# Single PSUM banks in place of pairs for the Fourier products, a third bank for the W_in product, and later uses of what went through DRAM

## The chip, the cores and the metric

One core of a Trainium2 chip runs the kernel as one program. The metric is the device time of one execution in microseconds (us); the kernel before takes 2753.14 us in the median of three runs. TensorE is the matmul engine, VectorE (DVE), ScalarE (ACT) and GpSimd (POOL) work on tiles, and SyncE (SP) issues most of the DMAs. PSUM is the accumulator memory: eight banks of 512 fp32 columns on 128 partitions.

## What is computed

A Fourier layer feeds a mixture-like MLP. With x of 8 batches, 3008 positions and 256 channels, and F = 2048:

```python
X = np.fft.rfft(x, axis=1)
Yr = Xr @ w_r - Xi @ w_i + b_r
Yi = Xr @ w_i + Xi @ w_r + b_i
Yr = np.sign(Yr) * np.maximum(np.abs(Yr) - lam, 0.0)
Yi = np.sign(Yi) * np.maximum(np.abs(Yi) - lam, 0.0)
y = np.fft.irfft(Y, n=x.shape[1], axis=1)
h = y @ w_in
g = h * np.cos(h)
out = g @ w_out
```

## The kernel before, in words

3008 is 64 x 47, so the real transform is done as two small ones (64 and 47 points, the latter padded to 48). For one batch the Fourier layer has three stages. stage_a (L354) makes the 64-point transform, tile pa, and sends it to DRAM (scr1). stage_b (L383) reads it back (tile at) in four quarters q: f2t1 (L410) makes the 47-point transform pb and splits it into a high and a low part Xh, Xl; wmix (L472) makes the three products pw with the Fourier weights, adds, clips, and at its end calls fold (L540) for both halves e, which combines rows on GpSimd, transposes on VectorE and sends the result through DRAM (scrT) into y; inverse, that is spread (L574), makes the 47-point inverse pi and stores it to DRAM (scr2). stage_c (L661) reads 1/6 of that back (tile bt), makes the 64-point inverse pc and evicts it as xTh and xTl, the input of the MLP.

The MLP (moe_step, L707) goes over 6 tiles t of 512 positions (the last 448) and 16 blocks f of 128 of the 2048 features. Each step has six matmuls into ph (h), ScalarE and VectorE make u = h cos h, gh and gl are its high and low part, and three steps later `second` (L689) adds six matmuls into two banks o0 and o1. It is 12 matmuls a step, 96 steps a batch.

The Fourier work of batch b + 1 and b + 2 is mixed into the MLP of batch b. The generators yield a cost; pull() (L817) runs after each half step and takes as much of the generator `ahead` (L779) as a fixed rate allows. The rate of tile t is (C_COST + share)/15/2 per pull, with C_COST = 5.22 and share = (A_COST + B_COST)/4.8 = 62.36/4.8. The yields inside stage_b stand for time that a DRAM round trip takes: 3.5 at its start, 2.0 ahead of wmix(0) (L649), 2.0 ahead of inverse(3) (L655); GAP = 5 units stand ahead of stage_c(b + 1, 0) (L799), and 3.5 between the load and the products of stage_c (L671). From this program the framework makes a fixed order for each engine: it takes instructions by the program's order, but puts a later one first where an earlier one is not expected to be ready; a buffer or bank is handed out when its first user is placed. `high_priority` moves an instruction to the front, `issue_after` keeps instructions behind a given one.

PSUM: tag f has two tiles of two banks each (`pair`, L284), for pa, pb, pw, pi and pc; tag h has two single banks for ph; o0 and o1 one each. The prologue's single tiles go round over six places, f, h, o0, f, h, o1 (fps, L276). pa and pi come in quartets: four small fp32 products, of two halves h of the input rows and two halves v of the output rows, that fill a pair and run side by side on the array (burst, L287); h says which bank.

Of the kernel before, what the change touches and what calls it, by code (L numbers as in the profile page):

```python
# [12 lines left out]
F32 = mybir.dt.float32  # L13
# [5 lines left out]
ALU = mybir.AluOpType  # L19
# [18 lines left out]
F2_COST = 0.43  # L38
GAP = 5
A_EVERY, A_FIRST = 3, 13  # L40
A_PAIR = 1.15
# [99 lines left out]
def tile_body(ctx: ExitStack, tc, x, w_r, w_i, b_r, b_i, w_in, w_out,  # L141
              c_f2, c_sig, c_f3, c_ff, c_if, c_iw, c_sgn, out):
    nc = tc.nc
# [210 lines left out]
    def stage_a(b):  # L354
        scr1[b] = dr.tile([32, 2, 2, 24, 256], F32, tag="scr1", name=f"scr1_{b}")
        ld = {}

        def load(c):
            if c < 12:
                ld[c] = stage_in("xt")  # L360
                with tc.issue_after(mark["f0", 2].ins) if b == 1 else ExitStack():
                    nc.sync.dma_start(ld[c], x[b, :, 512 * c:512 * (c + 1)])

        for c in range(2):
            load(c)
        yield 0.0
        yield 1.0
        for cc in range(6):
            p = pair("pa")
            xs = [ld.pop(2 * cc + v) for v in range(2)]  # L370
            burst([((p[64 * v:64 * v + 64, h], ff[64 * h:64 * h + 64, 256:], xs[v][64 * h:64 * h + 64]),
                    dict(start=True, stop=True, skip_group_check=True)) for v in (1, 0) for h in range(2)])
            ao = stage_out("ao")
            nc.scalar.copy(ao, p.rearrange("p h x -> p (h x)"))
            for v in range(2):
                i = 4 * cc + 2 * v
                nc.sync.dma_start(scr1[b][:, :, :, i:i + 2].rearrange("s r g i d -> (s r) g (i d)"),
                                  ao[64 * v:64 * v + 64].rearrange("p (g x) -> p g x", g=2))
                load(2 * cc + 2 + v)
            yield A_PAIR  # L380


    def stage_b(b):  # L383
# [26 lines left out]
        def f2t1(q):  # L410
# [10 lines left out]
            for hf in range(4):  # L421
# [11 lines left out]
                if b:  # L433
                    at = ld.pop(u)
                    if hf % 2 == 0:
                        p = pair("pb")
                    pv = p[:, hf % 2, :384].rearrange("p (s r c k) -> p s r c k", s=2, r=2, c=2)
                    for j in range(2):
                        for c in range(2):
                            mm(pv[:, j, :, c], at[:, j, 128 * c:128 * c + 128], f2[:, 2 * (hf % 2) + j],  # L440
                               start=j == 0 and c == 0, stop=j == 1 and c == 1, skip_group_check=True)
                    if hf % 2 == 0:
                        continue
                    pv = p[:, :, :384]
                    xhv, xlv = (a[:, 2 * hf - 2:2 * hf + 2].rearrange("p (u s) g k -> p u (s g k)", u=2) for a in (xh, xl))
# [26 lines left out]
        def wmix(q):  # L472
# [3 lines left out]
            if b:  # L476
                k1 = wk.tile([128, 2, 8, 48], F32, tag="k1", name="k1", bufs=1)
                for wj, comp in ((0, 2), (1, 0), (2, 1)):
                    p = pair("pw")
                    for e in range(2):  # L480
                        es = slice(128 * e, 128 * e + 128)
                        for c in range(2):
                            xhv, xlv = (x[comp][c] for x in xs)
                            mm(p[:, e, :384], wf[:, wj, 0, c, es], xhv, start=c == 0, stop=False)  # L484
                            mm(p[:, e, :384], wf[:, wj, 1, c, es], xhv, start=False, stop=False)  # L485
                            mm(p[:, e, :384], wf[:, wj, 0, c, es], xlv, start=False, stop=c == 1)  # L486
                    p4 = p[:, :, :384].rearrange("p e (s k) -> p e s k", k=48)
                    if wj == 0:
                        nc.scalar.copy(k1, p4)
                        yield 2.0  # L490
                        continue
                    r = 2 - wj
                    sv = st[:, :, :, r, :]
                    if r:
                        nc.vector.tensor_tensor(out=sv, in0=p4, in1=k1, op=ALU.add)
                    else:
                        nc.vector.tensor_tensor(out=sv, in0=k1, in1=p4, op=ALU.subtract)
                    cl = wk.tile([128, 2, 8, 48], F32, tag="cl", name="cl", bufs=1)
                    for e in range(2):
                        nc.vector.tensor_scalar(out=cl[:, e], in0=sv[:, e], scalar1=blo[:, r, e:e + 1],  # L500
                                                scalar2=bhi[:, r, e:e + 1], op0=ALU.max, op1=ALU.min)
                    nc.vector.tensor_tensor(out=sv, in0=sv, in1=cl, op=ALU.subtract)
                    yield 2.0
                for e in range(2):
                    fold(q, e)
                return
            for e in range(2):
                es = slice(128 * e, 128 * e + 128)
                k1 = wk.tile([128, 8, 48], F32, tag="k1", name="k1", bufs=1)
                for wj, comp in ((0, 2), (1, 0), (2, 1)):  # L510
                    p = fps("pw")
                    pv = p[:, :384]
                    for c in range(2):
                        mm(pv, ws[wj][:, 256 * c + 128 * e:256 * c + 128 * e + 128],
                           xs[:, comp, c].rearrange("p s k -> p (s k)"), start=c == 0, stop=c == 1)
                    p3 = pv.rearrange("p (s k) -> p s k", k=48)
                    if wj == 0:
                        nc.scalar.copy(k1, p3)
                        yield 1.0
                        continue  # L520
                    r = 2 - wj
                    sv = st[:, e, :, r, :]
                    if r:
                        nc.vector.tensor_tensor(out=sv, in0=p3, in1=k1, op=ALU.add)
                    else:
                        nc.vector.tensor_tensor(out=sv, in0=k1, in1=p3, op=ALU.subtract)
                    cl = wk.tile([128, 8, 48], F32, tag="cl", name="cl", bufs=1)
                    if q < 3 and r == 0:
# [7 lines left out]
                    (nc.gpsimd if q < 3 else nc.vector).tensor_tensor(out=sv, in0=sv, in1=cl, op=ALU.subtract)  # L536
                    yield 1.0
        Y = {}
# [35 lines left out]
        def spread(q):  # L574
            y = Y.pop(q).rearrange("p (a s e) -> p a s e", a=8, s=8)
            for u in range(2):
                p = pair("pi")
                burst([((p[64 * v:64 * v + 64, h], iw[64 * h:64 * h + 55],
                         y[64 * h:64 * h + 55, :, 4 * u + 2 * v:4 * u + 2 * v + 2]),
                        dict(start=True, stop=True, skip_group_check=True)) for v in range(2) for h in (1, 0)])  # L580
                bo = stage_out("bo")
                for h in range(2):
                    nc.scalar.copy(bo[:, 512 * h:512 * h + 512].rearrange("p (s a e) -> p s a e", s=2, a=8),
                                   p[:, h].rearrange("p (a s e) -> p s a e", s=2, a=8))
# [64 lines left out]
        yield 2.0  # L649
# [5 lines left out]
        yield 2.0  # L655
# [5 lines left out]
    def stage_c(b, t):  # L661
# [10 lines left out]
        p = pair("pc")  # L672
        for hf in range(2):
            for j in range(2):
                for c in range(2):
                    o = 256 * j + 128 * c
                    mm(p[:, hf, o:o + 128], bt[:, 2 * hf + j, 128 * c:128 * c + 128], ff[:, 128:256], start=o == 0, stop=o == 384,  # L677
                       skip_group_check=True)
# [97 lines left out]
    B_COST = 4 * (8 * F2_COST + 6 * 1.0 + 2 * A_PAIR) + 7.5  # L776
# [88 lines left out]
```

## Time and profile before

| what | value |
|---|---|
| runs | 2750.15, 2753.14, 2754.5 us |
| profiled execution | 2753.34 us, of it a span of 2751.6 us from the first to the last instruction |
| TensorE busy | 2673.5 us (97%), mean granted clock 0.991 |
| VectorE, ScalarE, GpSimd busy | 1763.5, 1670.5, 988.7 us |
| TensorE idle | 78.1 us, the span less the busy time |

TensorE's records overlap: a matmul of 512 columns is recorded with about 390 ns, but the next one starts 0.23 us after it, and that distance is what a matmul costs. An fp32 product (pa, pb, pi, pc) has two records, one for each of its passes. A wait is listed as the idle time of an engine just before an instruction, with what ended it.

### The profile page before, as it was taken

To read this page: it belongs to the slowest core of one execution; us is meant where nothing else is said; L and a number is where in the kernel's file an instruction comes from. 1 tells how busy PE (TensorE), PEld (TensorE's weight loads), DVE (VectorE), ACT (ScalarE), POOL (GpSimd) and SP (SyncE) were. 2 spreads that over 40 slices of the span, in tenths; PEclk is the share of its full clock that TensorE was granted. 3 is DMA by queue.
4 is the path that set the end of the run, shared out by engine and by line. 5 is a ranking of instruction groups with operands and counts; after the bars stand their busy time and mean duration, and the time that the engine had idled before them with its cause. 6 is when DMAs were issued, how large, how long until landed. Compare 5 with 4: busy or idle time off the path is not lost.

```text
span 2751.6 us, 36096 instructions
## 1 busy us (share of the span) xinstructions
PE 2673.5 (97%) x13161; PEld 2186.7 (79%) x13161; DVE 1763.5 (64%) x2640; ACT 1670.5 (61%) x2846; POOL 988.7 (36%) x907
## 2 busy tenths in 40 slices
PE   8789999999999999999999999999999999999999
PEld 6467778878788877977878787887878778788888
DVE  6586565666666666666656666566665666666665
ACT  5465556666566656666666666666665555666666
POOL 4354343443233432444324343243423434222222
PEclk9999999999999999999999999999999999999999
DMA  6523422343213432133322432223331222201000
GB/s 195 149 76 104 127 90 80 90 120 108 73 34 96 120 94 73 40 116 111 92 62 77 113 105 81 62 84 104 94 92 40 73 68 58 81 16 30 8 16 15
DMA packets 148051, 224.89 MB, mean 82 GB/s; under 512 B 13840, under 2 KB 91168, under 8 KB 147872
## 3 DMA queue, kind: packets, MB, share of 16 engines
q1 hardware_dynamic: 142592, 205.24, 25.9%
q0 software_dynamic: 5280, 17.33, 2.1%
q8 instruction: 104, 1.70, 0.3%
q14 instruction: 75, 0.61, 0.1%
HBM read 121.33 MB, written 101.19 MB: 81 GB/s over the span
## 4 chain that ended last, share of the span: by engine, by line
PE 81%; DMA 8%; DVE 6%; issue 2%; ACT 1%; POOL 1%; SPq 1%; ACTq 0%; DVEq 0%; POOLq 0%
PE po L696 11%; PE ph L714 11%; PE po L700 11%; PE ph L715 11%; PE ph L716 11%; PE po L697 11%; PE pc L677 3%; DMA scrT<-tr 3%; DMA y<-scrT 3%; PE pb L440 3%; PE pw L486 2%; PE pw L485 2%; PE pw L484 2%; PE pi L290 2%; PE pa L290 1%
## 5 line engine op out<-in xcount | busy, mean ns | idle before, releaser
L267 POOL TENSOR_TENSOR gl<-u,gh 128x512 fp32r<-128x512 f32 (+1 forms) x384 | 487.5, 1270 | 1379.4 <-ACT gh L726 1055.4
L722 DVE SCALAR_TENSOR_TENSOR u<-ph,u 128x512 f32<-128x512 f32 (+1 forms) x768 | 518.8, 676 | 500.8 <-ACT u L721 497.8
L721 ACT ACTIVATE u<-ph 128x512 int32<-128x512 f32 (+1 forms) x768 | 451.2, 588 | 461.7 <-PE ph L716 454.8
L725 DVE TENSOR_TENSOR u<-ph,u 128x512 f32<-128x512 f32 (+1 forms) x768 | 520.2, 677 | 262.4 <-ACT u L724 245.4
L724 ACT ACTIVATE u<-u 128x512 f32<-128x512 f32 (+1 forms) x768 | 479.9, 625 | 288.2 <-DVE u L722 285.2
L714 PE MATMUL ph<-xTh,win 128*128 128x512 f32 (+1 forms) x1536 | 608.5, 396 | 7.1 <-DVE u L725 5.7
L696 PE MATMUL po<-gh,wout 128*128 128x512 f32 (+1 forms) x1536 | 603.5, 393 | 0.1
L715 PE MATMUL ph<-xTl,win 128*128 128x512 f32 (+1 forms) x1536 | 595.6, 388 | 0.0
L716 PE MATMUL ph<-xTh,win 128*128 128x512 f32 (+1 forms) x1536 | 595.2, 388 | 0.0
L697 PE MATMUL po<-gh,wout 128*128 128x512 f32 (+1 forms) x1536 | 594.2, 387 | 0.0
L726 ACT CAST gh<-u 128x512 fp32r<-128x512 f32 (+1 forms) x768 | 467.9, 609 | 195.2 <-DVE u L725 190.2
L700 PE MATMUL po<-gl,wout 128*128 128x512 f32 (+1 forms) x1536 | 482.2, 392 | 4.4 <-DVE gl L270 4.2
L696 PEld LDWEIGHTS po<-gh,wout 128*128 128x128 f32 x1536 | 289.6, 189 | 90.0 <-ACT u L721 30.0
L714 PEld LDWEIGHTS ph<-xTh,win 128*128 128x128 f32 x1536 | 289.7, 189 | 80.4 <-DVE u L725 18.0
L270 DVE TENSOR_TENSOR gl<-u,gh 128x512 fp32r<-128x512 f32 (+1 forms) x384 | 310.1, 808 | 52.3 <-ACT gh L726 45.7
L700 PEld LDWEIGHTS po<-gl,wout 128*128 128x128 f32 x1536 | 281.2, 188 | 74.2 <-issue 8.9
L716 PEld LDWEIGHTS ph<-xTh,win 128*128 128x128 f32 x1536 | 289.5, 188 | 57.6 <-issue 0.8
L697 PEld LDWEIGHTS po<-gh,wout 128*128 128x128 f32 x1536 | 289.5, 188 | 51.4
L715 PEld LDWEIGHTS ph<-xTl,win 128*128 128x128 f32 x1536 | 290.0, 189 | 49.4 <-issue 0.8
L677 PEld LDWEIGHTS pc<-ff,bt 128*128 128x128 f32 x768 | 105.5, 200 | 36.2 <-issue 17.9
L677 PE MATMUL pc<-ff,bt 128*128 128x128 f32 x768 | 108.4, 285 | 25.4 <-DMA bt<-scr 25.4
L440 PEld LDWEIGHTS pb<-f,at 96*128 96x128 f32 x896 | 116.6, 191 | 8.4
(120 smaller groups left out, 2460.4 us busy)
## 6 DMA issues: line engine op xcount, KB each, us to landing
scrT<-tr SPq DMA_DIRECT2D x56, 512.0 KB, 2.9
y<-scrT SPq DMA_DIRECT2D x112, 256.0 KB, 5.1
scr<-bo SPq DMA_DIRECT2D x128, 192.0 KB, 2.9
bt<-scr SPq DMA_DIRECT2D x96, 256.0 KB, 3.8
xt<-in_dram SPq DMA_DIRECT2D x84, 256.0 KB, 3.9
scr<-ao SPq DMA_DIRECT2D x84, 256.0 KB, 3.5
at<-scr SPq DMA_DIRECT2D x112, 192.0 KB, 3.1
out_dram<-ob SPq DMA_DIRECT2D x80, 256.0 KB, 2.2
```

The source lines that it names most:

```text
L267: return nc.gpsimd.tensor_tensor(out=lo, in0=x, in1=hi.bitcast(F32), op=ALU.subtract)
L696: mm(po[e][:, :n], wo[0][:, 0, f, es], gh[:, :n], start=f == 0, stop=False)
L697: mm(po[e][:, :n], wo[0][:, 1, f, es], gh[:, :n], start=False, stop=False)
L700: mm(po[e][:, :n], wo[0][:, 0, f, es], gl[:, :n], start=False, stop=f == NFC - 1)
L714: mm(h, win[:, 0, c, fs], th[:, c, :n], start=c == 0, stop=False)
L715: mm(h, win[:, 0, c, fs], tl[:, c, :n], start=False, stop=False)
L716: mm(h, win[:, 1, c, fs], th[:, c, :n], start=False, stop=c == 1)
L721: nc.scalar.activation(k[:, :n], h, AF.Identity, bias=0.25, scale=1.0 / TWO_PI)
L722: nc.vector.scalar_tensor_tensor(out=u[:, :n], in0=h, scalar=1.0 / TWO_PI, in1=k[:, :n], op0=ALU.mult, op1=ALU.subtract)
L724: nc.scalar.activation(u[:, :n], u[:, :n], AF.Sin, bias=HALF_PI, scale=TWO_PI)
L725: nc.vector.tensor_tensor(out=u[:, :n], in0=h, in1=u[:, :n], op=ALU.mult)
L726: nc.scalar.copy(gh[:, :n], u[:, :n])
```

## The change

PSUM is dealt out anew: tag f gets three single banks and tag h three, o0 and o1 stay. Each of pa and pi is two single tiles, one for each h; pb and pc are one single tile for each hf, and pw one for each half e, each with its own evictions (two of 512 or 384 columns in place of one of 1024 or 768). In a quartet the order of the four products is by h first, then v; before it was by v first. The first matmul of a quartet is no longer at high priority, and outside the prologue it waits for the readers of the fourth-last f tile, which are noted by `drained`; the other three stay at high priority behind it. wmix of the later batches runs over e outermost, with fold(q, e) right after each e; k1 and cl have two buffers in place of one and half the size. The prologue's single tiles go round over eight places. The yields become 3.0 ahead of wmix(0), 5.0 ahead of inverse(3), GAP 7; B_COST grows by the same 4.0; A_EVERY is 5 in place of 3, as stage_b now yields more often.

```diff
-GAP = 5
-A_EVERY, A_FIRST = 3, 13
+GAP = 7
+A_EVERY, A_FIRST = 5, 13
...
     def fps(name):
-        if not banks:
-            banks.extend(("f", "h", "o0", "f", "h", "o1"))
-        tag = banks.pop(0)
-        if tag == "f":
-            return pair(name)[:, 0]
-        return ps.tile([128, 512], F32, tag=tag, name=name, bufs=1 if tag[0] == "o" else 2)
-
-    def pair(name):
-        return ps.tile([128, 2, 512], F32, tag="f", name=name, bufs=2)
+        if "pro" in pool:
+            if not banks:
+                banks.extend(("f", "h", "o0", "f", "h", "o1", "f", "h"))
+            tag = banks.pop(0)
+            return ps.tile([128, 512], F32, tag=tag, name=name, bufs=1 if tag[0] == "o" else 3)
+        p = ps.tile([128, 512], F32, tag="f", name=name, bufs=3)
+        ring.append((p, []))
+        return p
+
+    ring = []
+
+    def drained(p, ins):
+
+        for q, readers in ring[-6:]:
+            if q is p:
+                readers.append(ins.ins)
 
     def burst(calls):
 
-        with tc.high_priority():
-            ins = mm(*calls[0][0], **calls[0][1])
-            with tc.issue_after(ins.ins):
-                for a, k in calls[1:]:
-                    mm(*a, **k)
+        ins = mm(*calls[0][0], **calls[0][1])
+        if len(ring) > 3:
+            for r in ring[-4][1]:
+                tc.add_manual_dep(ins.ins, r.name, mybir.DependencyInfo(
+                    mybir.DependencyClass.Sync, mybir.DependencyReason.DATA), reason="bank")
+        with tc.high_priority(), tc.issue_after(ins.ins):
+            for a, k in calls[1:]:
+                mm(*a, **k)
...
-            p = pair("pa")
+            p = [fps("pa") for _ in range(2)]
...
-                    dict(start=True, stop=True, skip_group_check=True)) for v in (1, 0) for h in range(2)])
+                    dict(start=True, stop=True, skip_group_check=True)) for h in range(2) for v in (1, 0)])
             ao = stage_out("ao")
-            nc.scalar.copy(ao, p.rearrange("p h x -> p (h x)"))
+            for h in range(2):
+                drained(p[h], nc.scalar.copy(ao[:, 512 * h:512 * h + 512], p[h]))
...
-                    if hf % 2 == 0:
-                        p = pair("pb")
-                    pv = p[:, hf % 2, :384].rearrange("p (s r c k) -> p s r c k", s=2, r=2, c=2)
+                    p = fps("pb")
+                    pv = p[:, :384].rearrange("p (s r c k) -> p s r c k", s=2, r=2, c=2)
...
                     nc.scalar.copy(xhv, pv)
-                    nc.vector.tensor_tensor(out=xlv, in0=pv, in1=xhv.bitcast(F32), op=ALU.subtract)
-                    yield 4 * F2_COST
+                    drained(p, nc.vector.tensor_tensor(out=xlv, in0=pv, in1=xhv.bitcast(F32), op=ALU.subtract))
+                    if hf % 2:
+                        yield 4 * F2_COST
                     continue
...
-            if b:
-                k1 = wk.tile([128, 2, 8, 48], F32, tag="k1", name="k1", bufs=1)
-                for wj, comp in ((0, 2), (1, 0), (2, 1)):
-                    p = pair("pw")
...
-                for e in range(2):
-                    fold(q, e)
-                return
             for e in range(2):
                 es = slice(128 * e, 128 * e + 128)
-                k1 = wk.tile([128, 8, 48], F32, tag="k1", name="k1", bufs=1)
+                k1 = wk.tile([128, 8, 48], F32, tag="k1", name="k1", bufs=2)
...
+                        xhv, xlv = (x[comp][c] for x in xs)
+                        mm(pv, wf[:, wj, 0, c, es], xhv, start=c == 0, stop=False)
+                        mm(pv, wf[:, wj, 1, c, es], xhv, start=False, stop=False)
+                        mm(pv, wf[:, wj, 0, c, es], xlv, start=False, stop=c == 1)
...
                     yield 1.0
+                if b:
+                    fold(q, e)
...
-                p = pair("pi")
+                p = {h: fps("pi") for h in (1, 0)}
...
-                        dict(start=True, stop=True, skip_group_check=True)) for v in range(2) for h in (1, 0)])
+                        dict(start=True, stop=True, skip_group_check=True)) for h in (1, 0) for v in range(2)])
...
-        yield 2.0
+        yield 3.0
         yield from wmix(0)
...
-        yield 2.0
+        yield 5.0
         yield from inverse(3)
...
-        p = pair("pc")
         for hf in range(2):
+            p = fps("pc")
...
-        pv = p.rearrange("p f (j c n) -> p c (f j) n", j=2, c=2)
-        thv, tlv = (a.rearrange("p c (i n) -> p c i n", i=4) for a in (th, tl))
-        nc.scalar.copy(thv, pv)
-        nc.vector.tensor_tensor(out=tlv, in0=pv, in1=thv.bitcast(F32), op=ALU.subtract)
+            pv = p.rearrange("p (j c n) -> p c j n", j=2, c=2)
+            thv, tlv = (a[:, :, 256 * hf:256 * hf + 256].rearrange("p c (j n) -> p c j n", j=2) for a in (th, tl))
+            nc.scalar.copy(thv, pv)
+            drained(p, nc.vector.tensor_tensor(out=tlv, in0=pv, in1=thv.bitcast(F32), op=ALU.subtract))
...
-        ph = ps.tile([128, 512], F32, tag="h", name="ph", bufs=2)
+        ph = ps.tile([128, 512], F32, tag="h", name="ph", bufs=3)
...
-    B_COST = 4 * (8 * F2_COST + 6 * 1.0 + 2 * A_PAIR) + 7.5
+    B_COST = 4 * (8 * F2_COST + 6 * 1.0 + 2 * A_PAIR) + 11.5
```

## Rows read from the trace of the kernel before

**Rows 1.** The page: busy us, share of the span, instructions of each engine.
```profile
PE 2673.5 (97%) x13161; PEld 2186.7 (79%) x13161; DVE 1763.5 (64%) x2640; ACT 1670.5 (61%) x2846; POOL 988.7 (36%) x907
```

**Rows 2.** Stretches: busy us of each engine over one batch, granted clock, DMA.
```profile
core 0: us, PE busy (x) PEld busy (x) DVE busy (x) ACT busy (x) POOL busy (x), PEclk, DMA share, GB/s
...
780.00:1110.00 330.00, 326.73 (x1631) 267.58 (x1630) 213.41 (x318) 202.12 (x344) 122.67 (x112) 1.00 0.30 87
```

**Rows 3.** TensorE's waits, whole run: us in total, times, longest.
```profile
PE pc L677 <- DMA bt<-scr: 25.4, 8, 11.4
PE pi L290 <- DMA y<-scrT: 18.5, 12, 3.7
PE ph L714 <- DVE u L725: 5.7, 8, 1.6
PE po L700 <- DVE gl L270: 4.2, 4, 1.2
...
PE pi L619 <- ACT bo L622: 1.4, 1, 1.4
```

**Rows 4.** Stretches at half clock in the steady part: first, last, sum of six.
```profile
302.70:306.10 3.40, 3.40 (x11) 2.83 (x12) 0.28 (x1) 1.59 (x3) 3.05 (x2) 0.50 0.27 61
...
2381.40:2384.90 3.50, 3.50 (x16) 3.31 (x16) 0.62 (x1) 0.62 (x1) 1.27 (x1) 0.51 0.02 5
sum 23.90, PE 23.60 PEld 18.49 DVE 3.12 ACT 6.99 POOL 9.60; mean PE 3.93 PEld 3.08 DVE 0.52 ACT 1.16 POOL 1.60
```

**Rows 5.** Timelines of SP's queue and of PE around one bt wait.
```profile
1066.95 1.27 SPq L669 DMA_DIRECT2D bt<-scr  x2
...
1069.35 0.39 PE L716 MATMUL ph<-xTh,win 128*128 128x512 f32 x1
1071.93 1.80 PE L677 MATMUL pc<-ff,bt 128*128 128x128 f32 x14 [2.20 <-DMA bt<-scr]
```

**Rows 6.** Timelines of PE and ACT: a pc group, later work, its eviction.
```profile
1080.65 1.95 PE L677 MATMUL pc<-ff,bt 128*128 128x128 f32 x16
...
1111.79 1.92 PE L440 MATMUL pb<-f,at 96*128 96x96 f32 x16
...
1158.11 1.01 ACT L681 CAST xTh<-pc 128x1024 fp32r<-128x1024 f32 x1
```

**Rows 7.** Timelines of PE and its weight loads around one quartet.
```profile
1003.82 0.39 PE L715 MATMUL ph<-xTl,win 128*128 128x512 f32 x1
...
1004.04 0.39 PE L716 MATMUL ph<-xTh,win 128*128 128x512 f32 x1
...
1004.36 0.64 PE L290 MATMUL pi<-y,iw 55*64 55x512 f32 x1
1004.37 0.14 PEld L293 LDWEIGHTS pi<-y,iw 55*64 55x64 f32 x3
1004.37 0.65 PE L293 MATMUL pi<-y,iw 55*64 55x512 f32 x3
...
1004.84 0.59 PE L290 MATMUL pi<-y,iw 55*64 55x512 f32 x1
...
1005.38 0.50 PE L696 MATMUL po<-gh,wout 128*128 128x512 f32 x1
```

**Rows 8.** TensorE's y waits in 450 to 2103 us, then in 2103 to 2440 us.
```profile
PE pi L290 <- DMA y<-scrT: 4.1, 5, 1.1
...
PE pi L290 <- DMA y<-scrT: 9.4, 4, 3.7
```

**Rows 9.** Groups by shape of ACT and DVE: busy us, mean ns of one.
```profile
L583 ACT COPY bo<-pi 128x512 f32<-128x512 f32 x112 | 59.3, 583 | 13.5 <-PE pi L293 13.4
...
L374 ACT COPY ao<-pa 128x1024 f32<-128x1024 f32 x42 | 42.3, 1007 | 3.7 <-PE pa L293 3.6
...
L725 DVE TENSOR_TENSOR u<-ph,u 128x512 f32<-128x512 f32 x640 | 440.5, 688 | 218.7 <-ACT u L724 205.8
...
L682 DVE TENSOR_TENSOR xTl<-pc,xTh 128x1024 fp32r<-128x1024 f32 x48 | 58.8, 1224 | 13.8 <-ACT xTh L681 13.8
```

**Rows 10.** Groups by shape of PE: the first product of each quartet, two records each.
```profile
L290 PE MATMUL pi<-y,iw 55*64 55x512 f32 x112 | 60.4, 621 | 18.5 <-DMA y<-scrT 18.5
L290 PE MATMUL pa<-xt,ff 64*64 64x512 f32 x84 | 44.9, 614 | 1.1 <-DVE Xl L447 1.1
```

More of the change, by code (lines that the diff above doesn't have):

```diff
@@ L368, in stage_a @@
         for cc in range(6):
-            p = pair("pa")
+            p = [fps("pa") for _ in range(2)]
             xs = [ld.pop(2 * cc + v) for v in range(2)]
-            burst([((p[64 * v:64 * v + 64, h], ff[64 * h:64 * h + 64, 256:], xs[v][64 * h:64 * h + 64]),
-                    dict(start=True, stop=True, skip_group_check=True)) for v in (1, 0) for h in range(2)])
+            burst([((p[h][64 * v:64 * v + 64], ff[64 * h:64 * h + 64, 256:], xs[v][64 * h:64 * h + 64]),
+                    dict(start=True, stop=True, skip_group_check=True)) for h in range(2) for v in (1, 0)])
             ao = stage_out("ao")
-            nc.scalar.copy(ao, p.rearrange("p h x -> p (h x)"))
+            for h in range(2):
+                drained(p[h], nc.scalar.copy(ao[:, 512 * h:512 * h + 512], p[h]))
             for v in range(2):
@@ L441, in f2t1 @@
                                start=j == 0 and c == 0, stop=j == 1 and c == 1, skip_group_check=True)
[L442 to L445, printed above, removed]
+                    pv = p[:, :384]
+                    xhv, xlv = (a[:, 2 * hf:2 * hf + 2].rearrange("p s g k -> p (s g k)") for a in (xh, xl))
                     nc.scalar.copy(xhv, pv)
-                    nc.vector.tensor_tensor(out=xlv, in0=pv, in1=xhv.bitcast(F32), op=ALU.subtract)
-                    yield 4 * F2_COST
+                    drained(p, nc.vector.tensor_tensor(out=xlv, in0=pv, in1=xhv.bitcast(F32), op=ALU.subtract))
+                    if hf % 2:
+                        yield 4 * F2_COST
                     continue
@@ L475, in wmix @@
             ST[q] = st
-            if b:
-                k1 = wk.tile([128, 2, 8, 48], F32, tag="k1", name="k1", bufs=1)
-                for wj, comp in ((0, 2), (1, 0), (2, 1)):
-                    p = pair("pw")
-                    for e in range(2):
[L481 to L489, printed above, removed]
-                        yield 2.0
[L491 to L502, printed above, removed]
-                    yield 2.0
-                for e in range(2):
-                    fold(q, e)
-                return
             for e in range(2):
                 es = slice(128 * e, 128 * e + 128)
-                k1 = wk.tile([128, 8, 48], F32, tag="k1", name="k1", bufs=1)
+                k1 = wk.tile([128, 8, 48], F32, tag="k1", name="k1", bufs=2)
                 for wj, comp in ((0, 2), (1, 0), (2, 1)):
@@ L513, in wmix @@
                     for c in range(2):
-                        mm(pv, ws[wj][:, 256 * c + 128 * e:256 * c + 128 * e + 128],
-                           xs[:, comp, c].rearrange("p s k -> p (s k)"), start=c == 0, stop=c == 1)
+                        if b == 0:
+                            mm(pv, ws[wj][:, 256 * c + 128 * e:256 * c + 128 * e + 128],
+                               xs[:, comp, c].rearrange("p s k -> p (s k)"), start=c == 0, stop=c == 1)
+                            continue
+                        xhv, xlv = (x[comp][c] for x in xs)
+                        mm(pv, wf[:, wj, 0, c, es], xhv, start=c == 0, stop=False)
+                        mm(pv, wf[:, wj, 1, c, es], xhv, start=False, stop=False)
+                        mm(pv, wf[:, wj, 0, c, es], xlv, start=False, stop=c == 1)
                     p3 = pv.rearrange("p (s k) -> p s k", k=48)
                     if wj == 0:
-                        nc.scalar.copy(k1, p3)
+                        drained(p, nc.scalar.copy(k1, p3))
                         yield 1.0
@@ L523, in wmix @@
                     if r:
-                        nc.vector.tensor_tensor(out=sv, in0=p3, in1=k1, op=ALU.add)
+                        i = nc.vector.tensor_tensor(out=sv, in0=p3, in1=k1, op=ALU.add)
                     else:
-                        nc.vector.tensor_tensor(out=sv, in0=k1, in1=p3, op=ALU.subtract)
-                    cl = wk.tile([128, 8, 48], F32, tag="cl", name="cl", bufs=1)
-                    if q < 3 and r == 0:
+                        i = nc.vector.tensor_tensor(out=sv, in0=k1, in1=p3, op=ALU.subtract)
+                    drained(p, i)
+                    cl = wk.tile([128, 8, 48], F32, tag="cl", name="cl", bufs=2)
+                    if b == 0 and q < 3 and r == 0:
                         nc.scalar.activation(cl, sv, AF.Relu, bias=blo[:, r, e:e + 1], scale=-1.0)
@@ L535, in wmix @@
                                             op0=ALU.max, op1=ALU.min)
-                    (nc.gpsimd if q < 3 else nc.vector).tensor_tensor(out=sv, in0=sv, in1=cl, op=ALU.subtract)
+                    (nc.gpsimd if b == 0 and q < 3 else nc.vector).tensor_tensor(out=sv, in0=sv, in1=cl, op=ALU.subtract)
                     yield 1.0
+                if b:
+                    fold(q, e)
         Y = {}
@@ L576, in spread @@
             for u in range(2):
-                p = pair("pi")
-                burst([((p[64 * v:64 * v + 64, h], iw[64 * h:64 * h + 55],
+                p = {h: fps("pi") for h in (1, 0)}
+                burst([((p[h][64 * v:64 * v + 64], iw[64 * h:64 * h + 55],
                          y[64 * h:64 * h + 55, :, 4 * u + 2 * v:4 * u + 2 * v + 2]),
-                        dict(start=True, stop=True, skip_group_check=True)) for v in range(2) for h in (1, 0)])
+                        dict(start=True, stop=True, skip_group_check=True)) for h in (1, 0) for v in range(2)])
                 bo = stage_out("bo")
-                for h in range(2):
-                    nc.scalar.copy(bo[:, 512 * h:512 * h + 512].rearrange("p (s a e) -> p s a e", s=2, a=8),
-                                   p[:, h].rearrange("p (a s e) -> p s a e", s=2, a=8))
+                for h in (1, 0):
+                    drained(p[h], nc.scalar.copy(bo[:, 512 * h:512 * h + 512].rearrange("p (s a e) -> p s a e", s=2, a=8),
+                                                 p[h].rearrange("p (a s e) -> p s a e", s=2, a=8)))
                 for v in range(2):
@@ L648, in stage_b @@
             return
-        yield 2.0
+        yield 3.0
         yield from wmix(0)
@@ L654, in stage_b @@
             yield from wmix(q)
-        yield 2.0
+        yield 5.0
         yield from inverse(3)
@@ L676, in stage_c @@
                     o = 256 * j + 128 * c
-                    mm(p[:, hf, o:o + 128], bt[:, 2 * hf + j, 128 * c:128 * c + 128], ff[:, 128:256], start=o == 0, stop=o == 384,
+                    mm(p[:, o:o + 128], bt[:, 2 * hf + j, 128 * c:128 * c + 128], ff[:, 128:256], start=o == 0, stop=o == 384,
                        skip_group_check=True)
-        pv = p.rearrange("p f (j c n) -> p c (f j) n", j=2, c=2)
-        thv, tlv = (a.rearrange("p c (i n) -> p c i n", i=4) for a in (th, tl))
-        nc.scalar.copy(thv, pv)
-        nc.vector.tensor_tensor(out=tlv, in0=pv, in1=thv.bitcast(F32), op=ALU.subtract)
+            pv = p.rearrange("p (j c n) -> p c j n", j=2, c=2)
+            thv, tlv = (a[:, :, 256 * hf:256 * hf + 256].rearrange("p c (j n) -> p c j n", j=2) for a in (th, tl))
+            nc.scalar.copy(thv, pv)
+            drained(p, nc.vector.tensor_tensor(out=tlv, in0=pv, in1=thv.bitcast(F32), op=ALU.subtract))
         yield 1.72
```

## The prediction, made before the changed kernel was run

> **What bounds the kernel now.** I read the page's busy shares first, then the same by stretches, then TensorE's waits. TensorE is busy 97% of the span; the next engine, VectorE, 64% [rows 1]. In a whole batch of the steady part, 330 us, TensorE is busy 326.7 us and the granted clock is 1.00 [rows 2]: 3.3 us are idle. So no change of PSUM can win more than TensorE's waits and what they cost in clock. The list of waits [rows 3] gives the inventory: 25.4 us for bt, 18.5 us for y, 5.7 us for VectorE to free an h bank (ph), 4.2 us for gl. Of the 25.4 us, 11.4 us is one wait at the end of the prologue, where no other work exists yet and which no edit touches; seven waits of 14.0 us remain. Six stretches at a granted clock of 0.50, that is 1.2 in place of 2.4 GHz, lie behind the longer of these waits, three behind bt and three behind y; they last 23.9 us together [rows 4], and work at half speed loses half of that, 12.0 us. The whole prize of the steady part is therefore 14.0 + 18.5 + 5.7 + 4.2 + 12.0 = 54.4 us.
>
> How such a wait arises is seen at 1071.93 [rows 5]: the bt load is issued at 1066.95, TensorE starts its last ph matmul at 1069.35, and the next instruction in its fixed order is pc, 2.20 us before the data are there. The order was fixed when the program was written; it is a little too early for the DMA.
>
> One more fact decides about the banks. The pc products of 1080.65 are evicted at 1158.11, 77 us later [rows 6] (the groups of pc and their evictions pair off in order), because their xT buffer is still in use. They run far ahead of need, and hold one pair of f banks meanwhile. There are 48 such evictions [rows 9], one after another, so the rest of the Fourier work mostly lives on the other pair.
>
> **The change, part by part.** The sum is made against the profiled execution: 2753.34 us, 2751.6 of it span; it stands 0.2 us above the median 2753.14.
>
> *More work between store and use.* A pull of the planner is worth (5.22 + 62.36/4.8)/30 = 0.607 units before and (5.22 + 66.36/4.8)/30 = 0.635 after; two pulls are one step of 12 matmuls, 12 x 0.227 = 2.7 us (a ph product starts 0.22 to 0.23 us after the one before [rows 7]). GAP from 5 to 7 units is from 4.1 to 5.5 steps, 3.8 us more ahead of stage_c(b+1, 0); the longest steady bt wait is 2.4 us. The yield ahead of inverse(3), 2.0 to 5.0, is from 1.6 to 3.9 steps, 6.2 us more; the y waits of five middle batches are 4.1 us together, none over 1.1 [rows 8]. I take the seven bt waits as gone, -14.0, and these y waits, -4.1. The other seven y waits (14.4 us, up to 3.7 [rows 8]) lie in the first and the seventh batch, mostly between quarters where no yield is added, but fold(q, 0) now stands ahead of the second half of the W products. All that it issues moves with it: four GpSimd operations (eight in the first quarter), four transposes on VectorE and one scrT store on SP. Each then stands ahead of work of the next MoE step on its queue, gl on GpSimd, u on VectorE, the out store on SP, and holds it up where its own input isn't ready; behind gl wait the po products. Bounds 0 to -14.4; I take half, -7.2. The clock goes with the waits: three stretches behind bt, 10.3 us, give back 5.1; half of the 13.6 us behind y give back 3.4; -8.5 together. Should no wait go, this part is worth 0.
>
> *Three h banks.* The ph wait of 5.7 us (eight waits, all in the first batch) should nearly go, as a third bank is one step of slack: -5; bounds 0 and -5.7. The gl wait stays.
>
> *Single tiles.* Each eviction of two banks becomes two. On ScalarE one copy of 1024 columns is 1007 ns, one of 512 is 583 [rows 9]: 0.16 us more per pair, for 42 pa, 56 pb, 28 k1 and 48 pc some 28 us. VectorE's 1224 against 2 x 688 ns [rows 9] is 0.15 us, for pb, pc and the two W results 160 times, some 24 us, and as much again at most for the 56 clip subtractions. At 61% and 64% of the span [rows 1] this hides behind TensorE: 0; without that cover it would be 28 us. The extra semaphore work on TensorE's queue shows in no row; from the 0.01 us between matmuls of a quartet [rows 7] it is under 5 us for all.
>
> *Prologue.* Eight rotating banks in place of six. TensorE's waits for a ScalarE eviction there are short, 1.4 us the longest [rows 3]; -2, bounds +3 and -5.
>
> *Quartets.* This is the part that can cost. A quartet stands for 1.11 us of TensorE: from the start of the last ph product, 1004.04, to the first po, 1005.38, less one matmul of 0.23 [rows 7]. It is that short because all four small products of a pass run at once. Now its two banks are two tiles. The new wait is on the first matmul, for the readers of the fourth-last Fourier tile. TensorE takes its work in order, so if that wait is late in the real run, all ph and po behind it wait, and ScalarE and VectorE after them. And it names the right bank only if banks are handed out in turn; [rows 6] show that they are not: pb goes on at 1111.79, in the other pair, while pc sits on its own. If pc holds two of three f banks, a quartet gets its second bank only after its own first half is copied out, and runs as two halves of 1.11 us each. There are (112 + 84)/2 = 98 quartets [rows 10], 92 outside the prologue: between 0 and +102 us. I take one in six, 15 x 1.11 = +17, nearer to none: with a third h bank TensorE's order needs less filling with Fourier work from far ahead, so pc should run ahead less, and where it doesn't hold banks the three rotate as the wait assumes.
>
> Inside the quartet the order changes too, to two products of the same half h in succession. In [rows 7] the three later weight loads and matmuls start 0.01 us after the first, among them the third in the order, which has the first one's h: the same rows of the array are no obstacle. The Trainium skill (TensorE: Matmul & The Clock Gate, Part 3, "What overlaps and what doesn't") says that a weight load overlaps running matmuls only when its row group differs. By that rule the new order would take two turns a pass and the sum would come to +70 in place of -24; the trace goes against the rule here. The sum has 0 for the order.
>
> Sum: -14.0 - 4.1 - 7.2 - 8.5 - 5 - 2 + 17 = -23.8, so 2753.3 - 23.8 = 2729.5, call it 2729.
>
> **The rivals.**
> A (forecast): the waits go, few quartets split: 2702 (hardly a split, all y waits gone) to 2746.
> B: the waits move with the work. The place in the order could follow from when data are expected, not from the program's place: pc runs tens of us ahead of use [rows 6], yet waits for its load [rows 5], so extra yields may shift nothing. Then only ph's 5 us go: 2748, and with a few splits 2755. Against it: added yields do shift the place of everything that isn't ahead.
> C: pc goes on running ahead and holds two of the three f banks, so quartets split. From 41/1.11 = 37 split quartets on, the gain is used up. With half of the 92 split, 51 us, and half of the gains gone, it is 2753 + 51 - 20 = 2784; with all split and no gain 2855. For it: the 77 us of [rows 6]. Against it: less run-ahead with three h banks.
> D: the same-row order makes products take turns: a pass is 0.48 us, 1004.36 to 1004.84 [rows 7], so each quartet's two passes take 0.96 us more, 98 x 0.96 = +94, with the gains 2753 + 94 - 41 = 2806. This is what the rule of the Trainium skill (TensorE: Matmul & The Clock Gate, Part 3) would do; [rows 7] speak against it.
>
> **How the numbers follow.** A 0.52, B 0.17, C 0.28, D 0.03. This kernel's runs lie within 0.16% of each other, so a change under 0.2% (5.5 us) can't be told from none. A is faster (0.52); B gives 0.02 faster, 0.13 same, 0.02 slower; C and D are slower, 0.31. Together 0.54, 0.13, 0.33. The predicted time is A's, 2729, with A's own range 2702 to 2746. The full range reaches up to half-split quartets, 2790, and leaves out the worse half of C, D and a little of A's lower edge.
>
> **What would show it.** Right: steady bt waits and the middle batches' y waits absent from TensorE's list; fewer stretches at 0.50; no ph wait; quartets of eight records side by side, still about 1.1 us; the time from pc to its xTh copy shorter than 77 us. Wrong: quartets recorded in two groups of four with po or ph between them (C); the four starts of a quartet no longer within 0.03 us (D); bt and y waits as before (B); or new waits of pa, pi or pw for a ScalarE or VectorE eviction, which would be the three banks as the bound.

## The result and the profile after

The changed kernel takes 2719.72 us in the median of four runs, against 2751.64 us for the kernel before beside it: a ratio of 0.9886, 95% interval 0.9868 to 0.9904. It is faster by 1.1%, or 32 us; forecast were 24 us. The profiled execution has a span of 2719.1 us, against 2751.6.

The page's busy shares of the kernel after, to be held against [rows 1]:

```profile
PE 2664.1 (98%) x13161; PEld 2185.7 (80%) x13161; DVE 1792.8 (66%) x2856; ACT 1679.0 (62%) x3020; POOL 989.1 (36%) x907
```

TensorE has as many instructions as before. It is idle for 55.0 us in place of 78.1, so 23.1 us of the 32.5 us of span are waits that went. VectorE and ScalarE have 216 and 174 instructions more, and 29 and 9 us more work; in the list below TensorE's waits for them behind the prologue are shorter than in [rows 3], so this work hides.

TensorE's waits in the kernel after (us in total, times, longest), to be held against [rows 3]:

```profile
PE pi L296 <- DMA y<-scrT: 17.0, 16, 3.7
PE pc L665 <- DMA bt<-scr: 13.4, 1, 13.4
PE pa L296 <- ACT bo L610: 2.7, 1, 2.7
PE ph L702 <- DVE u L713: 2.6, 2, 2.3
...
PE po L688 <- DVE gl L270: 0.3, 1, 0.3
```

All seven steady bt waits are gone; the one that is left is the prologue's, 13.4 us in place of 11.4. The gl waits are gone too but for 0.3 us, the ph waits halved. But y still costs 17.0 us, in more and shorter waits. Where they are, first in 137 to 450 us, then in the stretches of [rows 8], 450 to 2103 and 2103 to 2440 us:

```profile
PE pi L296 <- DMA y<-scrT: 7.6, 3, 3.7
...
PE pi L296 <- DMA y<-scrT: 8.3, 12, 1.2
...
PE pi L296 <- DMA y<-scrT: 1.2, 1, 1.2
```

In the middle batches the y waits have doubled, from 4.1 to 8.3 us. In the first batch they rose too, from 5.0 to 7.6; only in the seventh did they fall, from 9.4 to 1.2.

The stretches of the steady part at half clock, to be held against [rows 4] (us, busy time of the five engines, granted clock, DMA):

```profile
149.10:152.50 3.40, 3.40 (x10) 2.53 (x9) 3.40 (x6) 3.40 (x7) 1.42 (x2) 0.50 0.13 27
313.00:316.40 3.40, 3.40 (x10) 2.62 (x9) 1.38 (x2) 1.58 (x3) 0.00 (x0) 0.50 0.29 66
425.60:429.00 3.40, 3.40 (x10) 2.71 (x9) 0.69 (x1) 1.93 (x4) 0.00 (x0) 0.50 0.16 36
sum 10.20, PE 10.20 PEld 7.85 DVE 5.48 ACT 6.91 POOL 1.42; mean PE 3.40 PEld 2.62 DVE 1.83 ACT 2.30 POOL 0.47
```

10.2 us in place of 23.9: half of the difference, 6.9 us, comes back.

The greatest change is not in the list of waits. A pc group (its start, and its end) and its eviction in the timelines of TensorE and of ScalarE, the counterpart of [rows 6]:

```profile
1193.19 0.38 PE L665 MATMUL pc<-ff,bt 128*128 128x128 f32 x2
...
1199.18 1.50 PE L665 MATMUL pc<-ff,bt 128*128 128x128 f32 x12
...
1200.64 1.08 ACT L669 CAST xTh<-pc 128x512 fp32r<-128x512 f32 x2
```

xTh is copied right behind the last product, 7.5 us after the first one; before it was 77 us. From the last pc matmul of a tile to the start of its copy it is 47 us in the median before and 0.9 us after. Summed over all groups, pc sat in PSUM like this for 2418 us in pairs of banks before and for 671 us in single banks after. The work no longer runs far ahead of its place, but for the last batch: there the last eight of the 96 halves take 405 of the 671 us, up to 78 us each.

A quartet in TensorE's timeline, the counterpart of [rows 7]:

```profile
1413.03 0.64 PE L296 MATMUL pi<-y,iw 55*64 55x512 f32 x1
1413.04 0.65 PE L303 MATMUL pi<-y,iw 55*64 55x512 f32 x3
1413.51 0.59 PE L296 MATMUL pi<-y,iw 55*64 55x512 f32 x1
1413.52 0.60 PE L303 MATMUL pi<-y,iw 55*64 55x512 f32 x3
1414.05 0.50 PE L702 MATMUL ph<-xTh,win 128*128 128x512 f32 x1
...
1413.04 0.14 PEld L303 LDWEIGHTS pi<-y,iw 55*64 55x64 f32 x3
1413.08 0.13 PEld L296 LDWEIGHTS pi<-y,iw 55*64 55x64 f32 x1
```

It is whole, and takes 1.02 us from its first start to the next product, as before. In the whole trace two groups of four records stand alone, one split quartet of 98.

### The profile page after: what moved, and what is told of

The parts are those of the page before. It is cut to its first block, busy times and chain, and to the rows that moved or that the text cites. A ratio compares the mean times of both kernels' runs of the same rounds, so it can differ in the third digit from the quotient of the medians.

```text
span 2719.1 us, 36553 instructions
## 1 busy us (share of the span) xinstructions
PE 2664.1 (98%) x13161; PEld 2185.7 (80%) x13161; DVE 1792.8 (66%) x2856; ACT 1679.0 (62%) x3020; POOL 989.1 (36%) x907
## 4 chain that ended last, share of the span: by engine, by line
PE 79%; DMA 7%; DVE 7%; ACT 2%; issue 2%; SPq 1%; POOL 1%; ACTq 0%; POOLq 0%; DVEq 0%
PE ph L702 11%; PE ph L704 11%; PE ph L703 11%; PE po L685 11%; PE po L688 11%; PE po L684 11%; DMA y<-scrT 4%; PE pc L665 3%; PE pb L450 2%; PE pi L296 2%; PE pw L497 2%; PE pw L499 2%; PE pw L498 2%; DMA scrT<-tr 2%; DVE cl L519 1%
## 5 line engine op out<-in xcount | busy, mean ns | idle before, releaser
L270 DVE TENSOR_TENSOR gl<-u,gh 128x512 fp32r<-128x512 f32 (+1 forms) x384 | 303.4, 790 | 78.9 <-ACT gh L714 76.3
L704 PEld LDWEIGHTS ph<-xTh,win 128*128 128x128 f32 x1536 | 289.1, 188 | 67.0 <-issue 11.4
L665 PEld LDWEIGHTS pc<-ff,bt 128*128 128x128 f32 x768 | 108.5, 193 | 23.1 <-issue 14.2
L665 PE MATMUL pc<-ff,bt 128*128 128x128 f32 x768 | 109.6, 277 | 13.4 <-DMA bt<-scr 13.4
```

The lines of the kernel that those rows point to most:

```text
L704: mm(h, win[:, 1, c, fs], th[:, c, :n], start=False, stop=c == 1)
```

## The experiments

From the profile after, the theory was: the third h bank lets the MLP supply TensorE without gaps, so the Fourier work is no longer pulled ahead to fill them; it then sits at its place in the program, pc leaves its banks at once, and the bt waits go with that. The rival: the longer yields took the bt waits away, and the banks only let it happen.

**The old yields in the changed kernel.**

```diff
-GAP = 7
+GAP = 5
...
-        yield 3.0
+        yield 2.0
         yield from wmix(0)
...
-        yield 5.0
+        yield 2.0
         yield from inverse(3)
...
-    B_COST = 4 * (8 * F2_COST + 6 * 1.0 + 2 * A_PAIR) + 11.5
+    B_COST = 4 * (8 * F2_COST + 6 * 1.0 + 2 * A_PAIR) + 7.5
```

> The changed kernel with the old yields (2.0, 2.0, GAP 5, B_COST 7.5); banks and quartets as changed. Theory 1: the bt waits went because with three h banks the Fourier work no longer runs ahead of its place in the program, and the yields add little: the seven steady bt waits stay under 3 us together, the time is within 0.3% of the changed kernel's 2720, say 2722. Rival: the added yields took the bt waits away: about 14 us of bt waits return with some clock, 2735 to 2742.

Measured: 2754.83 us, ratio to the kernel before 1.0003 (0.9991 to 1.0016). The whole gain is gone, and both expectations fall: the time is even above the rival's, but the waits are others. TensorE's waits of this kernel, and then those in the middle batches, 450 to 2103 us:

```profile
PE pi L296 <- DMA y<-scrT: 33.7, 17, 3.6
PE pc L665 <- DMA bt<-scr: 13.5, 1, 13.5
...
PE pi L296 <- DMA y<-scrT: 25.3, 14, 3.6
```

No steady bt wait returned, as the theory had it. The y waits doubled to 33.7 us, some 2 us each: 25.3 us in the middle batches, where the kernel before has 4.1 and the changed one 8.3, and none in the seventh, so those waits went without the yields. Nine stretches at half clock lie behind the y waits; the first and the sum of their list:

```profile
308.60:312.10 3.50, 3.45 (x11) 1.61 (x12) 0.30 (x1) 1.44 (x3) 1.29 (x1) 0.51 0.01 4
...
sum 37.50, PE 35.01 PEld 21.25 DVE 7.31 ACT 17.45 POOL 7.74; mean PE 3.89 PEld 2.36 DVE 0.81 ACT 1.94 POOL 0.86
```

Against the kernel before: bt -14.0, ph and gl about -8, y +15.2, half of 13.6 us more at half clock +6.8. That is nothing on balance, and so is the time. (The profiled execution, 2746.48 us, is the quickest of this kernel's, which reach to 2763.5; the 7 us by which it is below the one before have no row here.)

**The new yields in the kernel before** (the same four lines the other way round, pairs and two h banks stay).

> The kernel before with the new yields alone (3.0, 5.0, GAP 7, B_COST 11.5); pairs and two h banks stay. Theory 1: the work still runs ahead, xTh follows pc by 30 to 76 us as before, bt and y waits stay at 12 to 16 and 17 to 20 us, 2748 to 2756. Rival (yields alone): the steady bt waits go, 14 us and the clock behind them, 2732 to 2738.

Measured: 2752.54 us, 1.0001 (0.9991 to 1.0010). TensorE's waits of this kernel:

```profile
PE pc L677 <- DMA bt<-scr: 26.7, 8, 11.7
PE pi L290 <- DMA y<-scrT: 18.5, 11, 3.3
...
```

They are those of [rows 3]. pc sat in PSUM for 2412 us, as before. Where work runs ahead, as here, a yield moves its place in the program and not its place in TensorE's order. So each half of the change alone is worth nothing, and the two together 1.1%.

**Two h banks in the changed kernel** (one PSUM bank unused).

```diff
-            return ps.tile([128, 512], F32, tag=tag, name=name, bufs=1 if tag[0] == "o" else 3)
+            return ps.tile([128, 512], F32, tag=tag, name=name, bufs=1 if tag[0] == "o" else 2 if tag == "h" else 3)
...
-        ph = ps.tile([128, 512], F32, tag="h", name="ph", bufs=3)
+        ph = ps.tile([128, 512], F32, tag="h", name="ph", bufs=2)
```

> The changed kernel with two h banks, one PSUM bank left unused. Theory 1: the Fourier work runs ahead again, pc holds two of three f banks for tens of us, quartets split into groups of four records (dozens of them), bt waits return: 2750 to 2800. Rival (single tiles, the bank wait and the yields did it, the third h bank only its few us of ph waits): xTh still follows pc by about 1 us, at most 10 split quartets, 2723 to 2728.

Measured: 2844.47 us, 1.0336 (1.0319 to 1.0353). The theory's mechanism, at more than its price. TensorE's waits of this kernel, and then a pc half with its eviction in the timelines of TensorE and ScalarE:

```profile
PE ph L702 <- DVE u L713: 23.2, 21, 3.6
PE pc L665 <- DMA bt<-scr: 21.1, 9, 13.3
PE pi L296 <- DMA y<-scrT: 18.5, 7, 4.4
PE po L688 <- DVE gl L270: 9.6, 18, 1.0
...
```

```profile
1118.57 1.05 PE L665 MATMUL pc<-ff,bt 128*128 128x128 f32 x8
...
1197.85 1.07 ACT L669 CAST xTh<-pc 128x512 fp32r<-128x512 f32 x2
```

pc is 79 us ahead again, 3867 us in all in single banks, and eight steady bt waits are back. 103 groups of four quartet records, one of twelve and 45 whole ones stand in the trace: about half of the quartets split. A group of four takes 1.10 us in the median, a whole one 1.11, so 52 splits cost some 57 us. TensorE's idle time grew from 55.0 to 93.6 us, 39 more, and the stretches at half clock from 10 to 44 us, 17 lost more: together 113 of the 119 us between the two profiled executions. This is the forecast's rival C, in a kernel with one h bank fewer. Four single f banks with two h banks were not run, so what single tiles in place of pairs do by themselves is open.

**Without the wait of a quartet's first matmul.**

```diff
-        if len(ring) > 3:
-            for r in ring[-4][1]:
-                tc.add_manual_dep(ins.ins, r.name, mybir.DependencyInfo(
-                    mybir.DependencyClass.Sync, mybir.DependencyReason.DATA), reason="bank")
```

> The changed kernel without the added wait of a quartet's first matmul. Theory 1: three f banks are enough when pc leaves them at once, but without the wait a quartet starts on one bank and splits: 10 to 40 quartets in groups of four, each 1.11 us more, 2730 to 2765. Rival: the wait never binds, since the banks are free by then: at most 5 split, 2718 to 2722.

Measured: 2773.28 us, 1.0071 (1.0054 to 1.0087); the theory's number of splits, at a time a little over its upper end. 67 groups of four and five of twelve stand in the trace, which is 36 split quartets; at 1.1 us each they are some 40 of the 51 us between the two profiled executions. One of them in TensorE's timeline:

```profile
1256.24 0.64 PE L296 MATMUL pi<-y,iw 55*64 55x512 f32 x1
1256.25 0.64 PE L299 MATMUL pi<-y,iw 55*64 55x512 f32 x1
1256.72 0.59 PE L296 MATMUL pi<-y,iw 55*64 55x512 f32 x1
1256.73 0.59 PE L299 MATMUL pi<-y,iw 55*64 55x512 f32 x1
1257.25 0.50 PE L680 MATMUL po<-gh,wout 128*128 128x512 f32 x1
...
1258.97 0.39 PE L699 MATMUL ph<-xTl,win 128*128 128x512 f32 x1
1259.29 1.08 PE L299 MATMUL pi<-y,iw 55*64 55x512 f32 x4
1260.30 0.44 PE L493 MATMUL pw<-Xh,wf 128*128 128x384 f32 x1
```

One bank's two products run, then a whole po and the start of a ph product, then the other bank's. Each half stands for as long as a whole quartet: 1.01 us from 1256.24 to 1257.25. pc sits for 671 us in all, as in the changed kernel, so pc is not what splits these quartets; whose banks they meet is open. In the changed kernel the only steady waits of a quartet's first matmul are those for y and one of 0.8 us, so the added wait costs next to nothing there, and without it the kernel is some 50 us slower.

**Order within the quartet as before.**

```diff
-                    dict(start=True, stop=True, skip_group_check=True)) for h in range(2) for v in (1, 0)])
+                    dict(start=True, stop=True, skip_group_check=True)) for v in (1, 0) for h in range(2)])
...
-                        dict(start=True, stop=True, skip_group_check=True)) for h in (1, 0) for v in range(2)])
+                        dict(start=True, stop=True, skip_group_check=True)) for v in range(2) for h in (1, 0)])
```

> The changed kernel with the four products of a quartet in the order of before (v first, then h). Theory (order within a quartet is free on the array): quartets start within 0.03 us in either order, waits as in the changed kernel, 2716 to 2724. Rival (taking turns by row group): the old order is quicker by up to 0.96 us a quartet, 2630 to 2700. Second rival (the first half's eviction gains from h first): old order slower by up to 0.2%, 2720 to 2726.

Measured: 2725.49 us, 0.9896 (0.9880 to 0.9913). The first pass of a quartet in TensorE's timeline of this kernel:

```profile
1224.26 0.64 PE L296 MATMUL pi<-y,iw 55*64 55x512 f32 x1
1224.27 0.65 PE L303 MATMUL pi<-y,iw 55*64 55x512 f32 x3
```

The starts are as near to each other as in the new order, and a quartet stands for 1.11 us in the median in both. The interval and the changed kernel's overlap for the greater part: no cost of the order shows, and the first rival falls. The second, a gain of some 0.2% from evicting the first half early, is neither shown nor excluded.

**Both folds last, as before.**

```diff
-                if b:
-                    fold(q, e)
+
+            if b:
+                for e in range(2):
+                    fold(q, e)
```

> The changed kernel with both folds after the second half of the W products, as before. Theory: the earlier fold shortens the last trip to y by the GpSimd and VectorE work of one fold, some 5 to 8 us, so without it the y waits grow from 17 to 30 to 50 us, with half-clock stretches: 2740 to 2765. Rival (the order adapts to it, as y is expected later): y waits 15 to 20 us, 2717 to 2724.

Measured: 2718.16 us, 0.9866 (0.9847 to 0.9885), no slower than with the early fold. The y waits of this kernel:

```profile
PE pi L296 <- DMA y<-scrT: 10.8, 17, 2.6
```

They are fewer than the 17.0 us of the changed kernel, and than the rival's 15 to 20. The theory falls: moving the fold ahead bought nothing.

**More yields.**

```diff
             yield from f2t1(q)
+            yield 1.5
             yield from inverse(q - 1)
...
-        yield 5.0
+        yield 7.0
         yield from inverse(3)
...
-    B_COST = 4 * (8 * F2_COST + 6 * 1.0 + 2 * A_PAIR) + 11.5
+    B_COST = 4 * (8 * F2_COST + 6 * 1.0 + 2 * A_PAIR) + 18.0
```

> The changed kernel with 1.5 more units ahead of each earlier inverse(q - 1) and 7.0 in place of 5.0 ahead of inverse(3), B_COST up by 6.5. Theory (the work now sits at its program place, so a yield moves it): of the 17 us of y waits some 12 go, with part of the 6.8 us at half clock, 2700 to 2710. Rival (the y waits follow when data are expected, whatever the yields): y waits 15 to 20 us, 2717 to 2724. Second rival (later Fourier work crowds the end of a batch): new waits of ph for xTh, over 2725.

Measured: 2700.03 us, 0.9805 (0.9790 to 0.9819), better than both kernels. TensorE's waits of this kernel:

```profile
PE pc L666 <- DMA bt<-scr: 14.0, 3, 13.0
PE pw L493 <- DVE Xf L466: 3.4, 1, 3.4
PE pi L296 <- DMA y<-scrT: 3.1, 2, 1.8
PE pi L296 <- DVE u L711: 3.1, 1, 3.1
...
```

By this list the y waits fell from 17.0 to 3.1 us. The wait of 3.1 us in the last row, put down to VectorE, is ahead of pi too: it ends at 2196.77, 0.14 us after the last part of y landed, so it may be another y wait. TensorE's idle time fell by 10.8 us, from 55.0 to 44.2, which fits 6.2 us of y waits better. The steady stretches at half clock fell from 10.2 to 6.8 us, 1.7 lost less: together 12.5 of the 15.1 us that the span lost.

**The three yields apart.** GAP 5 alone in the changed kernel (`GAP = 7` becomes `GAP = 5`):

> The changed kernel with GAP 5 in place of 7, all else as changed. Theory: GAP is not what took the bt waits away, as the run with all old yields had none: no steady bt wait, 2717 to 2724. Rival: bt waits of 1 to 2 us a batch return, 2730 to 2738.

Measured: 2722.77 us, 0.9886 (0.9871 to 0.9900), no steady bt wait: GAP alone shows no worth here. And the yield ahead of inverse(3) alone (5.0 becomes 2.0, B_COST + 8.5):

> The changed kernel with 2.0 in place of 5.0 ahead of inverse(3), B_COST with it; GAP 7 and the 3.0 ahead of wmix(0) stay. Theory (this yield alone is what the old-yields run lost): the seven y waits ahead of inverse(3) grow by some 2 us each with half-clock stretches behind them, y 28 to 36 us in all, 2743 to 2757. Rival (it takes all three yields, or the waits spread over others): y under 25 us, 2720 to 2735.

Measured: 2726.36 us, 0.9891 (0.9877 to 0.9904), y waits 16.7 us: no difference clear of the intervals. The theory falls. What the run with all old yields lost is in neither of these two; the yield ahead of wmix(0) alone, and pairs of them, were not tried.

**First matmul of a quartet at high priority again.**

```diff
-        ins = mm(*calls[0][0], **calls[0][1])
+        with tc.high_priority():
+            ins = mm(*calls[0][0], **calls[0][1])
```

> The changed kernel with the first matmul of each quartet at high priority again. Theory: at high priority a quartet goes to TensorE as soon as its data are expected, ahead of products that are ready, so y waits come more often and longer: 25 to 45 us in place of 17, with half-clock stretches, 2730 to 2755. Rival (the place is set by the yields alone): y waits 15 to 20 us, 2717 to 2726.

Measured: 2720.45 us, 0.9880 (0.9864 to 0.9897), y waits 17.5 us: no difference, the theory falls.

**Six places in the prologue, as before.**

```diff
-                banks.extend(("f", "h", "o0", "f", "h", "o1", "f", "h"))
+                banks.extend(("f", "h", "o0", "f", "h", "o1"))
```

> The changed kernel whose prologue's single tiles go round over the six places of before. Theory (the prologue is bound by loads and by evictions in the order of the data, not by banks): the first ph product starts within 2 us of the changed kernel's 139.2, 2717 to 2724. Rival (eight places give the prologue the 2 us of the prediction, or more): first ph 141 or later, 2721 to 2727.

Measured: 2725.15 us, 0.9894 (0.9881 to 0.9908). The first ph product comes at 143.6 us, against 139.2 in the changed kernel and 135.7 to 140.6 in the others that have its prologue. The rival is nearer: by this one execution eight places are worth some 3 us or more to this prologue, though the time shows no difference, and against the kernel before it starts the MLP no earlier (139.2 against 138.2).

**More yields and the folds last** (both edits above).

> The changed kernel with the longer yields of the run with more yields (1.5 ahead of each earlier inverse, 7.0 ahead of inverse(3)) and both folds last. Theory (the place of the folds matters little once the yields cover the trip): y waits under 5 us, 2695 to 2706. Rival (folds last make y later by one fold): y waits over 10 us, 2710 to 2720.

Measured: 2700.28 us, 0.9806 (0.9793 to 0.9819), y waits 4.8 us, no steady stretch at half clock in its profile. As the theory had it, the same as with more yields alone.

## Why the prediction was right, and where its steps were not

The direction and the size hold: 24 us forecast, 32 us measured, inside the range of case A. Of A's signs the steady bt waits, the stretches at half clock, the whole quartets and the time from pc to its copy came as forecast; the y waits of the middle batches, which were to be absent, doubled, and 2.6 us of ph waits stayed. That the sum lies so near is partly luck: the quartets came out 16 us better than summed and the y waits 10 us worse. Its steps, in us:

| step | forecast | measured |
|---|---|---|
| steady bt waits | -14.0 | -14.0 |
| y waits | -4.1 in the middle batches, -7.2 in the others | +4.2 in the middle batches, +2.6 in the first, -8.2 in the seventh |
| clock | -8.5 | -6.9 |
| ph waits | -5 | -3.1 |
| gl waits | 0 | -3.9 |
| prologue up to the first ph | -2 | +1.0 |
| split quartets | +17 (15 splits) | +1.1 (1 split) |

The measured column sums to -27 of the span's -32.5; where the rest is, no row here shows. The +1.0 of the prologue is no cost that can be told from none: among the runs with this prologue the first ph comes between 135.7 and 140.6 us.

*More work between store and use* was right for bt in size and wrong in cause. bt waits are away with the old yields too, stay with the new yields on the old banks, and come back with the running ahead when an h bank is taken: it is the end of running ahead that took them. For y the step failed where it counted the added 6.2 us ahead of inverse(3) against waits of 1.1 us, as the kernel before has them. On the new banks and the old yields the middle batches' y waits are 25.3 us, and the yields brought them to 8.3. Why they grow there was not tested; in the trace TensorE comes to pi sooner, for the second quarter of a middle batch 20 to 21 us after its last W product with the old yields, against 28 in the kernel before. The forecast treated banks and yields as a sum; they act together, and neither alone. What rival B says of added yields, that they may shift nothing, was true of the kernel before.

*The clock* step held in its mechanism, and -6.9 is near the -8.5. That the stretches lie behind "the longer" waits is too simple: in the kernel before one lies behind a bt wait of 1.8 us at 2381.0, and none behind the one of 2.20 us at 1071.93 [rows 5].

*The fold* was worth nothing (run with both folds last), where -7.2 was put down to it. The waits of the seventh batch go without the early fold and without the new yields: 1.1 us are left there with both folds last, none with the old yields.

*Three h banks* was the most mis-sized term: -5, for the ph wait alone. Without the third bank the changed kernel is 125 us slower. Its true work is that which the forecast named in passing, under the quartets, as a reason to expect few splits.

*Quartets* was right about the danger and its price: a half stands for 1.10 us as estimated (1.11), 52 quartets split with two h banks, 36 without the added wait. With both in place one quartet of 98 splits, and the +17 fell away. That the wait might name the wrong bank did not show.

*Single tiles* at 0 held: 29 us more on VectorE and 9 on ScalarE, where 28 were estimated, are hidden at 66% and 62%.

*The order within the quartet* at 0 held: four starts within 0.02 us of 1413.03 with two products of the same half in succession, and the next pass's weight loads at 1413.08 while they run. The rule of the Trainium skill (TensorE: Matmul & The Clock Gate, Part 3, "What overlaps and what doesn't"), that a weight load overlaps only with matmuls of another row group, does not hold in these rows, and rival D with it.

## What to carry to other kernels

Before adding delay ahead of a use that waits, look whether the work stands at its place in the program at all: the time from a product to its eviction (77 us against 7.5) tells it, and where it ran ahead here, yields moved nothing. Give the main loop enough banks first, so that TensorE's order needs no filling from far ahead; then every round trip needs its delay set anew: with more yields this kernel came to 2700.03 us. And keep products that share the array in one move: the wait for both banks cost next to nothing here, and the kernel without it is some 50 us slower.

## What the runs showed of the hardware

Two fp32 products on half of the array take as long as four on all of it: with two h banks, 1.10 us for a group of four records, 1.11 for one of eight.

TensorE's clock falls after quite short waits, but no length of a wait tells when. With the old yields it was granted 0.50, its lower level of 1.2 GHz, for 3.4 or 6.8 us behind nine y waits of 1.5 to 3.6 us, so that 33.7 us of y waits cost another 19 us of lost clock (an estimate, half of the 37.5 us); behind three others, of 1.6 to 2.2 us, it was not. The waits of up to 1.2 us in the middle batches of the kernel after have no such stretch behind them, yet with two h banks there is one behind a wait of 1.25 us, here in TensorE's timeline and the list of stretches:

```profile
2016.18 0.50 PE L702 MATMUL ph<-xTh,win 128*128 128x512 f32 x1 [1.25 <-DVE u L713]
...
2016.90:2020.30 3.40, 3.40 (x13) 1.04 (x11) 2.66 (x5) 2.60 (x5) 1.28 (x1) 0.50 0.00 0
```
